# One-hot products of two tokens instead of four, in a gated Fourier and expert mixture

## The chip, the cores and the metric

The kernel runs on one core of a Trainium2 chip. A core has TensorE (matrix products into the PSUM banks), VectorE, ScalarE and GpSimd for work on elements, and queues that issue DMAs, most of them on SyncE (SP). Each engine works through its own list of instructions in order and waits on semaphores for the others. The metric is the device time of one execution in microseconds (us). Where a rate is compared, a product is one instruction of TensorE, with a weight load before it.

## The reference

The output mixes two branches with a gate for each token. Both work on the same x of 2048 tokens by 640.

```python
g = _sigmoid((x * gate_w).sum(-1, keepdims=True))
a = _A_ref(x, ...)      # Real(DFT over tokens of DFT over channels), as four products with matrices
b = _B_ref(x, ...)      # experts
return g * a + (1 - g) * b
...
# _B_ref, for each token and each of 32 heads
s1, s2 = q1 @ k1.T, q2 @ k2.T            # 16 scores each
# the two best of each, the two best of the four sums: 2 of 16*16 = 256 experts
g = _softmax(top_s, axis=-1)
act = _gelu(x @ u[top_e])
out = sum over h, k of g * act * v[top_e]
```

The kernel doesn't gather experts. It computes x times all 256 rows of u, and needs for each token and each expert the sum of the gates of those heads that chose it: a table G of 16 x 16 for each token. G is what the changed part makes.

## The kernel before

The kernel has one order of instructions, written out by its Python code. The main loop runs over 128 pieces of the product with the sequence matrices (2 matrices, 4 blocks of 512 tokens out, 16 blocks of 128 tokens in). A piece is 15 products of a 128x128 stationary block with 512 columns (five blocks of channels, and three products for each, since every operand is split into a high and a low half to keep precision; lines 143 to 145). After the pieces come 84 steps of the product with the hidden matrices, of much the same kind.

All else is background work. The class `Pump` holds generators; after every three products `run_bg(0.68)` adds 0.95 x 0.68 us of credit, and while the credit is positive the next step of a generator is issued. What a step yields is its planned cost on VectorE, and is taken off the credit. Other work on VectorE takes credit away too (`bg.credit -= ...`). So the order on VectorE and ScalarE, relative to TensorE's, comes from these costs. The code sets `early` (piece below 92), `ending` (the last seven pieces) and `closing` (the last piece of a block of 512 tokens) for the background to read.

In the first pieces the loop also makes weights (`w_part`, line 380: products with 32 columns of weights and 320 elements that write the four quarters of the partitions), then the scores and their best two. The choices end up in `ROWS[g]`, two tiles for the two halves of the tokens (g = 0 and 1): for each half three rows, namely the power of two that stands for the first index, the same for the second, and the gate weight, with 128 partitions for heads, choices and the two halves of a weight, and a column for a token. `put_rows` (line 721) copies the last rows there; up to then `last_rows` holds them in a tile with the tag `xl`, the place of x^T's low half.

`experts` (line 802) makes G from them. A set is 64 tokens; a half of the tokens has 16 sets. For a set, `build` (line 836) writes two tiles of 1024 columns in float16: pt, the one-hot vectors of the first index times the weight, and qt, those of the second index. That is two comparisons of the rows with a table of powers of two (`wtab4`, 16 powers each repeated for four tokens) and a product with the weight (line 845, 128 x 1024 elements each). Columns are ordered as block m, power e, token t: a block is four tokens, 64 columns.

`use` (line 848) then issues a burst: for each set and each block of four tokens one product pt^T qt of 64 x 64 (line 857). Blocks go to partitions 0 to 63 and 64 to 127 in turn, and a set fills one PSUM bank of eight times 64 columns. Of a product only the entries where both tokens are the same are wanted. `mask` (line 815) multiplies every fourth column by a mask that is zero on the partitions of other tokens, in four instructions of ScalarE for a set; `add_up` (line 821) adds four columns on VectorE into `cd[g]`. `settle` does both for one set at each step of the background. When a half is summed, `store_gates` (line 793) stores it with two DMAs, from which the last part loads G.

The tiles for four sets (`HOT`, two tiles of two sets) are allotted once the scores' tiles are given back. A group is three sets, or two under `ending`. The loop at line 864 builds sets while one is free, and issues the burst of the group before when none is. So the first set of the next group is built ahead of each burst. The second tile of `HOT` has the tag `WP` and is given up at piece 124. The tag `xl` is used again from piece 95 on, by `load_parts`.

Of the kernel before, what the change touches and what calls it, by code (L numbers as in the profile page):

```python
# [17 lines left out]
P = 128  # L18
# [3 lines left out]
E = 16  # L22
# [17 lines left out]
NSTEP = 7 * KZ  # L40
AHEAD = 5
AWAY = 11
BYPASS = 4
ACCUM_END = NT * (NC + 2) - 4

# [61 lines left out]
def gated_mix_kernel(ctx: ExitStack, tc: tile.TileContext, xT, xn, dreT, dimT, wsre, wsim, wq, kT, uT, vv, gw, out):  # L107
# [94 lines left out]


    banks = []
    p3, last_part, ending, closing, early, share = None, False, False, False, True, 0.95
    grow, staged, P22 = {}, {}, {}

    def load_row(q):
# [130 lines left out]
    wtab4 = const.tile([P, E, 4], F16)  # L339
    powers = const.tile([P, E], F16)  # L340
    top_bits = const.tile([P, 1], F32)
    mask4 = const.tile([P, 4], F32)

    def put_keys():
        for r in range(2):
# [6 lines left out]
    def make_tables():  # L352
        for e in range(E):
            nc.gpsimd.memset(powers[:, e:e + 1], 2.0 ** (E - 1 - e))
        nc.gpsimd.memset(top_bits, INF)
        nc.gpsimd.tensor_copy(wtab4, powers[:, :, None].to_broadcast([P, E, 4]))
        nc.vector.tensor_reduce(mask4, identf.rearrange("p (a b) -> p b a", b=4), op=OP.add, axis=AX.X)
        nc.vector.tensor_scalar(mask4, mask4, 1.0 / GSCALE, None, op0=OP.mult)

    for n, f in ((2, put_keys), (4, make_ident), (9, make_tables)):  # L360
        at(n, f)
# [430 lines left out]

    def store_gates(g):
        if g in summed and g not in stored:
            for s in range(2):
                nc.sync.dma_start(gd[g][s].rearrange("t e f m -> e t f m"), summed[g][64 * s:64 * s + 64])
            stored.add(g)

    free_sets = deque(range(4))
# [2 lines left out]
    def experts():  # L802


        shp = [P, 16, E, 4]
        wt = wtab4[:, None].to_broadcast(shp)
        todo = deque((g, c) for g in range(2) for c in range(16))
        cd = {}

        masked, unmasked = deque(), deque()  # L810

        def mask(t):
            f = t.rearrange("p m (e t) -> p (m e) t", t=4)
            for n in range(4):
                nc.scalar.activation(f[:, :, n], f[:, :, n], AF.Copy, scale=mask4[:, n:n + 1])  # L815

        def add_up(g, c, t):
            if c == 0:
                store_gates(g - 1)
                cd[g] = p3.tile([P, E, P], F32, name="cd", tag="cd")  # L820
            nc.vector.tensor_reduce(cd[g][:, :, 8 * c:8 * c + 8].rearrange("p e m -> p m e"),
                                    t.rearrange("p m (e t) -> p m e t", e=E), op=OP.add, axis=AX.X)
# [12 lines left out]

        def build(g, c, s):
            pt, qt = (HOT[s // 2][:, s % 2, n].rearrange("p (m e t) -> p m e t", e=E, t=4) for n in range(2))

            def row(n):
                r = ROWS[g][:, n, 8 * c:8 * c + 8, :].rearrange("p b (s t) -> p (b s) t", t=4)  # L840
                return r[:, :, None, :].to_broadcast(shp)

            assert rowed >= set(range(8 * g, 8 * g + 8))
            for o, a, b, op in ((pt, row(0), wt, OP.is_equal), (qt, row(1), wt, OP.is_equal), (pt, pt, row(2), OP.mult)):
                nc.vector.tensor_tensor(o, a, b, op=op)  # L845
                yield (0.8 if early else 1.05) + settle()

        def use(group):
            assert not last_part
            while masked or unmasked:  # L850
                yield settle(True)
            for i, (g, c, s) in enumerate(group):
                t = bank((6, 7, 5)[i], (P, 8, E * 4))
                pt, qt = (HOT[s // 2][:, s % 2, n].rearrange("p (m c) -> p m c", m=16) for n in range(2))
                for m in range(16):
                    r = slice(64 * (m % 2), 64 * (m % 2) + 64)
                    nc.tensor.matmul(t[r, m // 2, :], pt[:, m], qt[:, m], start=True, stop=True)  # L857
# [372 lines left out]
    prep_split = {NPC - 4: (0,), NPC - 3: (1,), NPC - 2: (2,), NPC - 1: (3, 4)}  # L1230
    WP = None
    for n in range(N0, NPC):
        ending, closing, early = n >= NPC - 7, n % NT == NT - 1, n < ACCUM_END
        seq_piece(n)
        follow(n)
        if n >= N1 and p3 is None and NT // NB - 1 in gated:
            p2_stack.close()
            p3 = ctx.enter_context(tc.tile_pool(name="p3", bufs=1, reuse_waits="tile"))
            pools.append(p3)
            HOT.append(p3.tile([P, 2, 2, 16 * E * 4], F16, name="hot0"))  # L1240
            HOT.append(p3.tile([P, 2, 2, 16 * E * 4], F16, name="hot1", tag="WP"))
            bg.add(experts(), late=True)
            bg.credit -= 3.0
        if n == NPC - 4:
            bg.drain(lambda: {2, 3} <= set(free_sets))
            HOT.pop()
# [57 lines left out]
```

## Time and profile before

| | us |
|---|---|
| median of 3 runs | 750.32 (749.74 to 750.33) |
| profiled execution | 750.43 |
| its span, first to last instruction | 748.7 |
| TensorE busy | 743.8 |
| VectorE busy | 585.7 |
| ScalarE busy | 365.9 |
| GpSimd busy | 342.4 |

The profile is of one execution. A group of instructions is given by its line, engine, operation, the tile written and those read, and their shape; then its count, its busy time, the mean time of one in ns, and the idle time of the engine before it with what ended it. A product's duration is the time from its start to its modelled end; products overlap, so their starts tell the pace. The granted clock of TensorE has a mean of 0.999 over the span.

### The profile page before, as it was taken

Reading aid. Unit: us, or ns where it says so; the run is one execution under the profiler, and the core shown is the slowest. Engines: PE = TensorE matmul, PEld = TensorE weight load, DVE = VectorE, ACT = ScalarE, POOL = GpSimd, SP = SyncE. Lnnn points to the kernel's source line nnn. Section 1 sums busy time; section 2 is a strip of 40 time slices with the busy share of each in tenths; the row PEclk is TensorE's granted clock in tenths of the full one; section 3 lists DMA queues with packets and bytes.
Section 4 is the critical chain, followed back from the end, with each engine's and each line's share of the span. In section 5 each row is a group of like instructions: output and inputs, shape, how many; then the busy total and the mean of one; then the engine's idle time right before and its main releaser. Section 6 shows DMA issues by size and latency. Waiting matters only on the chain.

```text
span 748.7 us, 11141 instructions
## 1 busy us (share of the span) xinstructions
PE 743.8 (99%) x3925; PEld 603.8 (81%) x3925; DVE 585.7 (78%) x741; ACT 365.9 (49%) x664; POOL 342.4 (46%) x286
## 2 busy tenths in 40 slices
PE   9999999999999999999999999999999999999998
PEld 7777767888888888888888888888888888888887
DVE  6964098495999899999999888979899974357651
ACT  4325234543544745555463686633545653443451
POOL 5533325440532424145235456643455793487253
PEclk9999999999999999999999999999999999999999
DMA  9999999777556786972398766488876689775301
GB/s 333 392 380 364 344 374 354 231 222 250 129 176 141 190 242 157 237 200 79 114 395 285 162 168 188 133 255 280 266 234 197 222 262 343 219 239 172 113 29 71
DMA packets 84488, 171.11 MB, mean 229 GB/s; under 512 B 16080, under 2 KB 21328, under 8 KB 84176
## 3 DMA queue, kind: packets, MB, share of 16 engines
q1 hardware_dynamic: 70960, 146.13, 57.9%
q0 software_dynamic: 5472, 9.96, 8.5%
q10 hardware_dynamic: 8000, 14.31, 5.2%
q8 instruction: 31, 0.51, 0.3%
q14 instruction: 25, 0.20, 0.1%
HBM read 136.40 MB, written 32.39 MB: 225 GB/s over the span
## 4 chain that ended last, share of the span: by engine, by line
PE 94%; DMA 5%; SPq 0%; DVE 0%; ACT 0%; issue 0%; ACTq 0%
PE b L143 30%; PE b L145 30%; PE b L144 30%; PE b L239 2%; DMA wf<-in_wsre 2%; PE b L380 2%; DMA wq<-in_wq 1%; PE b L857 1%; DMA xd<-X 1%; DMA gdr<-gc 1%; DVE wp L386 0%; SPq L177 0%; ACT WS L295 0%; ACTq L514 0%; DVE ST L1191 0%
## 5 line engine op out<-in xcount | busy, mean ns | idle before, releaser
L143 PE MATMUL b<-WS,X 128*128 128x512 f32 x620 | 243.3, 392 | 0.0
L144 PE MATMUL b<-WS,X 128*128 128x512 f32 x620 | 241.4, 389 | 0.0
L145 PE MATMUL b<-WS,X 128*128 128x512 f32 x620 | 241.3, 389 | 0.0
L139 POOL TENSOR_TENSOR WS<-wf,WS 128x512 fp32r<-128x512 f32 x89 | 131.9, 1486 | 168.3 <-ACT WS L138 151.8
L143 PEld LDWEIGHTS b<-WS,X 128*128 128x128 f32 x620 | 116.3, 188 | 28.2 <-issue 4.1
L145 PEld LDWEIGHTS b<-WS,X 128*128 128x128 f32 x620 | 116.4, 188 | 24.4
L144 PEld LDWEIGHTS b<-WS,X 128*128 128x128 f32 x620 | 116.4, 188 | 23.6
L138 ACT ACTIVATE WS<-wf 128x512 fp32r<-128x512 f32 x89 | 55.5, 626 | 69.0 <-PE b L145 40.9
L845 DVE TENSOR_TENSOR hot<-rows,wtab 128x1024 f16<-128x1024 f16 x64 | 57.8, 930 | 4.3 <-PE b L857 4.3
L139 POOL TENSOR_TENSOR xl<-xf,xh 128x640 fp32r<-128x640 f32 x16 | 27.2, 1702 | 72.0 <-ACT xh L138 72.0
L567 ACT ACTIVATE sc<-b 128x512 f32<-128x512 f32 x32 | 19.9, 621 | 80.8 <-PE b L145 77.0
L191 POOL DMA_DIRECT2D WS<-in_wsre x30 | 26.4, 881 | 61.8 <-ACT WS L189 60.5
L139 POOL TENSOR_TENSOR WS<-ra,WS 128x512 fp32r<-128x512 f32 x33 | 47.1, 1439 | 14.3 <-ACT WS L138 14.1
L815 ACT ACTIVATE b<-b,mask 128x128 f32<-128x128 f32 x128 | 43.1, 342 | 14.9 <-PE b L857 11.8
L138 ACT ACTIVATE WS<-ra 128x512 fp32r<-128x512 f32 x47 | 29.4, 631 | 42.4 <-PE b L145 29.6
L622 DVE TENSOR_TENSOR eq<-sc,mm 128x1024 f16<-128x1024 f32 x32 | 44.4, 1387 | 0.9
L629 DVE TENSOR_REDUCE tied<-eq 128x64 f32<-128x1024 f16 x32 | 39.0, 1219 | 0.9
L620 DVE TENSOR_REDUCE mm<-sc 128x64 f32<-128x1024 f32 x32 | 38.7, 1211 | 0.2
L139 POOL TENSOR_TENSOR WP<-ra,WP 128x512 fp32r<-128x512 f32 x13 | 19.2, 1490 | 31.0 <-ACT WP L138 30.9
L217 DVE SCALAR_TENSOR_TENSOR ST<-ST,grow 128x512 f32<-128x512 f32 x40 | 31.7, 855 | 1.7 <-ACT tw L138 1.7
L845 DVE TENSOR_TENSOR hot<-hot,rows 128x1024 f16<-128x1024 f16 x32 | 31.6, 986 | 0.0
L143 PE MATMUL b<-WU,xh 128*128 128x512 f32 x80 | 31.1, 389 | 0.0
(209 smaller groups left out, 1449.1 us busy)
## 6 DMA issues: line engine op xcount, KB each, us to landing
X<-xd SPq DMA_DIRECT2D x36, 640.0 KB, 6.5
wq<-in_wq SPq DMA_DIRECT2D x32, 640.0 KB, 7.1
wf<-in_wsim SPq DMA_DIRECT2D x64, 256.0 KB, 4.8
wf<-in_wsre SPq DMA_DIRECT2D x63, 256.0 KB, 6.4
ra<-pd SPq DMA_DIRECT2D x40, 256.0 KB, 3.3
pd<-ST ACTq DMA_DIRECT2D x35, 256.0 KB, 5.6
WS<-in_wsre POOLq DMA_DIRECT2D x30, 256.0 KB, 6.0
xd<-X SPq DMA_DIRECT2D x11, 640.0 KB, 9.1
```

Source lines behind the costliest of these rows:

```text
L138: nc.scalar.activation(h, f, AF.Copy)
L139: eng.tensor_sub(l, f, h.bitcast(F32))
L143: nc.tensor.matmul(o, wh, ah, start=first, stop=False, skip_group_check=more)
L144: nc.tensor.matmul(o, wh, al, start=False, stop=False, skip_group_check=more)
L145: nc.tensor.matmul(o, wl, ah, start=False, stop=last, skip_group_check=more)
L191: nc.gpsimd.dma_start(l, (wsre, wsim)[w][c, s], accum_op=OP.add)
L217: nc.vector.scalar_tensor_tensor(f, f, -1.0 if w else 1.0, g, op0=OP.mult, op1=OP.mult)
L620: nc.vector.tensor_reduce(m, sc, op=OP.max, axis=AX.X)
L622: nc.vector.tensor_tensor(eq, sc, m[:, :, None].to_broadcast([P, HH, E]), op=OP.is_equal)
L629: nc.vector.tensor_reduce(tied[:, s, ib, :], eq, op=OP.add, axis=AX.X)
L815: nc.scalar.activation(f[:, :, n], f[:, :, n], AF.Copy, scale=mask4[:, n:n + 1])
L845: nc.vector.tensor_tensor(o, a, b, op=op)
```

## The change

A block is now two tokens (`TB = 2`). Products are 32 x 32, go to the four quarters of the partitions in turn (`CG = 4`), and there are 32 of them for a set (`MS`). Two sets fill a bank; the banks 5, 6 and 7 are taken in rotation. A mask has two instructions for a bank, each over 256 elements, and one sum covers a bank. A group is four sets, and always an even number. The half's result lies in four strips of 32 partitions, which four DMAs store. The builds' planned cost is 0.85 for 0.8 in the early part.

`HOT` becomes a list of sets, and a fifth may be added by `free_now`. For the first half of the tokens it is a tile with the tag `xl`, if all 16 rows have been put in place and `late` is not set (`late`: from piece 86 on). For the second half it lies in the first half's rows, `ROWS[0]`, which are no longer read then.

```diff
+TB = 2
+MS = 64 // TB
+CG = P // (TB * E)
...
-        nc.gpsimd.tensor_copy(wtab4, powers[:, :, None].to_broadcast([P, E, 4]))
-        nc.vector.tensor_reduce(mask4, identf.rearrange("p (a b) -> p b a", b=4), op=OP.add, axis=AX.X)
+        nc.gpsimd.tensor_copy(wtab, powers[:, :, None].to_broadcast([P, E, TB]))
+        nc.vector.tensor_reduce(mask_t, identf.rearrange("p (a b) -> p b a", b=TB), op=OP.add, axis=AX.X)
...
-            for s in range(2):
-                nc.sync.dma_start(gd[g][s].rearrange("t e f m -> e t f m"), summed[g][64 * s:64 * s + 64])
+            for s in range(CG):
+                n, t = divmod(TB * s, 4)
+                nc.sync.dma_start(gd[g][n, t:t + TB].rearrange("t e f m -> e t f m"),
+                                  summed[g][TB * E * s:TB * E * (s + 1)])
...
-        shp = [P, 16, E, 4]
-        wt = wtab4[:, None].to_broadcast(shp)
+        shp = [P, MS, E, TB]
+        wt = wtab[:, None].to_broadcast(shp)
...
         def mask(t):
-            f = t.rearrange("p m (e t) -> p (m e) t", t=4)
-            for n in range(4):
-                nc.scalar.activation(f[:, :, n], f[:, :, n], AF.Copy, scale=mask4[:, n:n + 1])
+            f = t.rearrange("p m (e t) -> p (m e) t", t=TB)
+            for n in range(TB):
+                nc.scalar.activation(f[:, :, n], f[:, :, n], AF.Copy, scale=mask_t[:, n:n + 1])
...
-            nc.vector.tensor_reduce(cd[g][:, :, 8 * c:8 * c + 8].rearrange("p e m -> p m e"),
+            nc.vector.tensor_reduce(cd[g][:, :, 8 * c:8 * c + 16].rearrange("p e m -> p m e"),
                                     t.rearrange("p m (e t) -> p m e t", e=E), op=OP.add, axis=AX.X)
-            if c == 15:
+            if c == 14:
                 summed[g] = cd[g]
...
+        def free_now():
+
+            if todo[0][0] == 1:
+                if not HOT[4:] or HOT[4][0] == 0:
+                    if HOT[4:] and 4 not in free_sets:
+                        return [s for s in free_sets if s < 2 or not ending]
+                    if not HOT[4:]:
+                        HOT.append(None)
+                        free_sets.append(4)
+                    HOT[4] = 1, ROWS[0].rearrange("p a b c -> p (a b c)")[:, :16 * P].rearrange("p (n c) -> p n c", n=2)
+            elif not HOT[4:] and not late and len(rowed) == NT:
+                HOT.append((0, big.tile([P, 2, 16 * P // 2], F16, name="hot4", tag="xl")))
+                free_sets.append(4)
+            return [s for s in free_sets if s not in ((2, 3) if ending else (4,) if late and todo[0][0] == 0 else ())]
+
+        def pair(s):
+            f = HOT[s][1] if s == 4 else HOT[s]
+            return f[:, 0], f[:, 1]
...
-                yield (0.8 if early else 1.05) + settle()
+                yield (0.85 if early else 1.05) + settle()
...
             for i, (g, c, s) in enumerate(group):
-                t = bank((6, 7, 5)[i], (P, 8, E * 4))
-                pt, qt = (HOT[s // 2][:, s % 2, n].rearrange("p (m c) -> p m c", m=16) for n in range(2))
-                for m in range(16):
-                    r = slice(64 * (m % 2), 64 * (m % 2) + 64)
-                    nc.tensor.matmul(t[r, m // 2, :], pt[:, m], qt[:, m], start=True, stop=True)
-                unmasked.append((g, c, t))
+                if i % 2 == 0:
+                    t = bank(5 + rotate("hot", 3), (P, 16, E * TB))
+                    unmasked.append((g, c, t))
+                pt, qt = (f.rearrange("p (m c) -> p m c", m=MS) for f in pair(s))
+                for m in range(MS):
+                    r = slice(TB * E * (m % CG), TB * E * (m % CG + 1))
+                    nc.tensor.matmul(t[r, 8 * (i % 2) + m // CG, :], pt[:, m], qt[:, m], start=True, stop=True)
...
-            while todo and len(group) < (2 if ending else 3):
-                free = [s for s in free_sets if s < 2 or not ending]
-                if prev and (not free or ending and any(s > 1 for g, c, s in prev)):
+            while todo and (len(group) < (2 if ending else 4) or len(group) % 2):
+                free = free_now()
+                if prev and (not free or ending and any(s in (2, 3) for g, c, s in prev)):
                     yield from use(prev)
...
-        ending, closing, early = n >= NPC - 7, n % NT == NT - 1, n < ACCUM_END
+        ending, closing, early, late = n >= NPC - 7, n % NT == NT - 1, n < ACCUM_END, n >= NT * (NC + 2) - 10
```

`HOT` is filled with four sets of the same two tiles as before, and at piece 124 sets 2 and 3 are taken out of it.

More of the change, by code (lines that the diff above doesn't have):

```diff
@@ L204, in gated_mix_kernel @@
     banks = []
-    p3, last_part, ending, closing, early, share = None, False, False, False, True, 0.95
+    p3, last_part, ending, closing, early, late, share = None, False, False, False, True, False, 0.95
     grow, staged, P22 = {}, {}, {}
@@ L338, in gated_mix_kernel @@
     identf = p1.tile([P, P], F32, name="identf", tag="uf", bufs=2)
-    wtab4 = const.tile([P, E, 4], F16)
+    wtab = const.tile([P, E, TB], F16)
     powers = const.tile([P, E], F16)
     top_bits = const.tile([P, 1], F32)
-    mask4 = const.tile([P, 4], F32)
+    mask_t = const.tile([P, TB], F32)
     def put_keys():
@@ L834, in settle @@
             return us
+        def free_now():
[14 more added lines that the diff above has]
+            return f[:, 0], f[:, 1]
         def build(g, c, s):
-            pt, qt = (HOT[s // 2][:, s % 2, n].rearrange("p (m e t) -> p m e t", e=E, t=4) for n in range(2))
+            pt, qt = (f.rearrange("p (m e t) -> p m e t", e=E, t=TB) for f in pair(s))
             def row(n):
-                r = ROWS[g][:, n, 8 * c:8 * c + 8, :].rearrange("p b (s t) -> p (b s) t", t=4)
+                r = ROWS[g][:, n, 8 * c:8 * c + 8, :].rearrange("p b (s t) -> p (b s) t", t=TB)
                 return r[:, :, None, :].to_broadcast(shp)
@@ L1232, in gated_mix_kernel @@
     for n in range(N0, NPC):
-        ending, closing, early = n >= NPC - 7, n % NT == NT - 1, n < ACCUM_END
+        ending, closing, early, late = n >= NPC - 7, n % NT == NT - 1, n < ACCUM_END, n >= NT * (NC + 2) - 10
+        assert n < NT * (NC + 2) - 1 or not HOT[4:] or HOT[4][0] or 4 in free_sets
         seq_piece(n)
@@ L1239, in gated_mix_kernel @@
             pools.append(p3)
-            HOT.append(p3.tile([P, 2, 2, 16 * E * 4], F16, name="hot0"))
-            HOT.append(p3.tile([P, 2, 2, 16 * E * 4], F16, name="hot1", tag="WP"))
+            for t in ("hot0", "WP"):
+                f = p3.tile([P, 2, 2, 16 * E * 4], F16, name="hot", tag=t)
+                HOT.extend(f[:, a] for a in range(2))
             bg.add(experts(), late=True)
```

4 lines of the change are left out of this document (2 added, 2 removed).

## The prediction

> **What bounds the kernel now.** I read the page first, then the list of TensorE's waits, then the timeline around the one-hot products of line 857.
>
> ```profile
> span 748.7 us, 11141 instructions
> PE 743.8 (99%) x3925; PEld 603.8 (81%) x3925; DVE 585.7 (78%) x741; ACT 365.9 (49%) x664; POOL 342.4 (46%) x286
> PEclk9999999999999999999999999999999999999999
> PE 94%; DMA 5%; SPq 0%; DVE 0%; ACT 0%; issue 0%; ACTq 0%
> L845 DVE TENSOR_TENSOR hot<-rows,wtab 128x1024 f16<-128x1024 f16 x64 | 57.8, 930 | 4.3 <-PE b L857 4.3
> L815 ACT ACTIVATE b<-b,mask 128x128 f32<-128x128 f32 x128 | 43.1, 342 | 14.9 <-PE b L857 11.8
> ...
> PE b L326 <- PEq L1296: 0.8, 1, 0.8
> PE b L380 <- DMA wq<-in_wq: 0.7, 1, 0.7
> ```
>
> TensorE is busy for 99% of the span at the full granted clock, and the chain that ended last is 94% TensorE. A busy TensorE need not run at its peak, so the list of its waits matters more: 0.8 us at the start, 0.7 us in the weight products, and nothing after that. In the stretch that the change touches (410 to 600 us) TensorE waits for no one. What VectorE and ScalarE save there is off the path; only two things can move the end: the time that the one-hot products hold TensorE, and a new wait of TensorE.
>
> **What a burst costs.** The next rows are the timeline of TensorE around the first burst of three sets, then around the last of two; columns are start, duration, line, form and count. The two rows under them are all products of line 857.
>
> ```profile
> 419.09 0.39 PE L144 MATMUL b<-WS,X 128*128 128x512 f32 x1
> 419.32 0.39 PE L145 MATMUL b<-WS,X 128*128 128x512 f32 x1
> 419.64 0.95 PE L857 MATMUL b<-hot 128*64 128x64 f16 x48
> 420.52 0.50 PE L143 MATMUL b<-WS,X 128*128 128x512 f32 x1
> 420.85 0.39 PE L144 MATMUL b<-WS,X 128*128 128x512 f32 x1
> ...
> 586.79 0.39 PE L145 MATMUL b<-WS,X 128*128 128x512 f32 x1
> 587.10 0.69 PE L857 MATMUL b<-hot 128*64 128x64 f16 x32
> 587.73 0.50 PE L143 MATMUL b<-WS,X 128*128 128x512 f32 x1
> 588.07 0.39 PE L144 MATMUL b<-WS,X 128*128 128x512 f32 x1
> ...
> L857 PEld LDWEIGHTS <-hot x512: 106/113/113, 419.6 to 587.6; 128*64 128x64 f16 x171
> L857 PE MATMUL b<-hot x512: 196/196/217, 419.6 to 587.6; 128*64 128x64 f16 x171
> ```
>
> Large products start 0.23 us apart. From the L145 before the first burst to the L144 after it are 1.53 us; without the burst these two starts would be 2 x 0.227 = 0.45 us apart, so a burst of 48 costs 1.08 us. The last, of 32, costs 1.28 - 0.45 = 0.83 us. The difference, 0.25 us, is 16 products: 15.7 ns a product, 31.4 ns for the two that lie side by side in the halves of the partitions. What is left, 1.08 - 48 x 0.0157 = 0.33 us, is paid once a burst, at the switch to small products and back. The 512 products are ten bursts of 48 and one of 32: 10 x 1.08 + 0.83 = **11.63 us**. This is all that the change can work on.
>
> **The new bursts.** 32 sets in fours make eight bursts. A set is now 32 products of 32 x 32 columns in place of 16 of 64 x 64, four side by side in the quarters of the partitions. No row shows such a product, so I bound four of them. If all the time is in columns, four take half of 31.4 ns: 15.7 ns. If what sets 31.4 ns is a fixed time for each strip, they take 31.4 ns. If the supply of instructions sets it, the only rate that the rows prove is 15.7 ns for a weight load and a product, so four take 62.8 ns. That four strips do overlap shows at line 380:
>
> ```profile
> 40.98 0.39 PE L145 MATMUL b<-WS,X 128*128 128x512 f32 x1
> 41.30 2.36 PE L380 MATMUL b<-wq,kp 128*32 128x320 f32 x32
> 43.59 0.50 PE L143 MATMUL b<-WS,X 128*128 128x512 f32 x1
> 43.93 0.40 PE L144 MATMUL b<-WS,X 128*128 128x512 f32 x1
> ```
>
> Here 2.95 - 0.45 - 0.33 = 2.17 us for 32 products 32 columns wide, 68 ns each for 320 elements; one large product spends 0.227 x 320 / 512 = 142 ns on as many. So strips of 32 run at least two at a time, and the switch in and out looks the same as for strips of 64 (43.59 to 43.93 as 420.52 to 420.85). I take the middle of the first two cases, 23.6 ns, as an estimate. A burst of four sets is 32 fours: 0.33 + 32 x 0.0236 = 1.09 us, eight are 8.7 us: **-2.9 us**. The ends are 8 x (0.33 + 0.50) = 6.7 us (-4.9), 8 x (0.33 + 1.00) = 10.7 us (-1.0) and 8 x (0.33 + 2.01) = 18.7 us (+7.1). The change breaks even at 11.63 / 8 - 0.33 = 1.12 us for 32 fours, 35 ns a four. A ninth burst, should the last sets come after the switch to groups of two, is +0.33.
>
> [...]
>
> **Masks, sums, tables.** The masks go from 128 instructions over 128 elements to 32 over 256; the sums from 32 to 16, each still over 512 elements.
>
> ```profile
> L567 ACT ACTIVATE sc<-b 128x512 f32<-128x512 f32 x32 | 19.9, 621 | 80.8 <-PE b L145 77.0
> L821 DVE TENSOR_REDUCE cd<-b x32: 678/681/696, 422.3 to 592.5; 128x128 f32<-128x512 f32 x32
> core 0: us, PE busy (x) PEld busy (x) DVE busy (x) ACT busy (x) POOL busy (x), PEclk, DMA share, GB/s
> 410.00:600.00 190.00, 190.00 (x1299) 155.56 (x1298) 172.13 (x217) 110.38 (x248) 101.56 (x73) 1.00 0.69 210
> L622 DVE TENSOR_TENSOR eq<-sc,mm 128x1024 f16<-128x1024 f32 x32 | 44.4, 1387 | 0.9
> ```
>
> A mask of 256 lies between 342 ns (128) and 621 ns (512): 0.43 us, 14 us in all for 43. VectorE loses 16 x 0.68 = 11 us. Both are worth nothing at the end, since TensorE doesn't wait there; they move the last sets earlier. The three comparisons and products of a set (line 845) keep their 1024 elements, in runs of two instead of four. I count no change; the other bound is the one-by-one 1.39 us of L622 against the free-running 0.68, +0.7 us x 96 = 68 us on an engine with 190 - 172 = 18 us free. The smaller tables are made in piece 9, beside the large products, as before. `store_gates` issues four DMAs for two.
>
> ```profile
> L796 SPq DMA_DIRECT2D gd<-cd x4: 527/547/637, 487.4 to 616.8; - x4
> L177 SPq DMA_DIRECT2D wf<-in_wsim x64: 327/382/1322, 316.0 to 572.8; - x64
> ```
>
> That is 2 x 0.55 us more on SP, once with the loads of `wf` queued behind it; these are issued five pieces (5 x 15 x 0.227 = 17 us) ahead. Cost nothing; uncovered, 1.1 us.
>
> **The fifth set, and the wait it should prevent.** With four sets and bursts of three, the set after the burst was built before the burst was issued, so VectorE had one set's lead. With four sets and bursts of four there is none: the burst stands right behind the last build. `free_now` gives a fifth set in the first half only when all 16 rows are in place and `late` is still off, that is before piece 86.
>
> ```profile
> 422.71 2.53 ACT L246 ACTIVATE ST<-b 128x512 f32<-128x512 f32 x5
> ...
> 452.60 0.63 ACT L189 ACTIVATE WS<-WS 128x512 fp32r<-128x512 f32 x1
> 453.14 1.93 ACT L721 ACTIVATE rows<-lb 128x384 f16<-128x384 f16 x1
> ...
> 420.52 0.68 DVE L845 TENSOR_TENSOR hot<-hot,rows 128x1024 f16<-128x1024 f16 x1
> ...
> 467.58 0.95 PE L857 MATMUL b<-hot 128*64 128x64 f16 x48
> ...
> 468.95 0.68 DVE L845 TENSOR_TENSOR hot<-hot,rows 128x1024 f16<-128x1024 f16 x1
> ```
>
> The copies at 422.71 empty the banks after piece 79, so piece 80 starts near 424.1 us, and piece 86 six pieces and two bursts later, near 424.1 + 6 x 3.4 + 2.2 = 446.7. The last row is copied at 453.14, behind a split (452.60) that piece 87 issues at about 450. So I expect that **the place in x^T's low half is never used**, and that the first half, four bursts, runs without a spare set. In the second half the first rows are the spare, and the lead is as before.
>
> What a missing lead costs is VectorE's lag. The first four sets were ready at 420.52 + 0.68 = 421.20; their burst would be issued about 0.6 us later than the first one now (12 builds cost 0.05 more in the pump's credit, over a share of 0.95), reaching its fourth set near 419.64 + 0.6 + 0.7 = 420.9: 0.3 us of waiting. The first 16 sets were ready at 469.63, 2.05 us after the burst at 467.58; less the same 0.7 and what the missing sums give back, about 0.5. Between them VectorE was less far behind. I take **+0.8 us** for the four; bounds 0 and 4 x 2.05 = 8.2. Behind a waiting product stands all of TensorE's queue, so such a wait is paid in full.
>
> **Sum.** Profiled execution: span 748.7 of 750.43 us, with 1.7 us around it. 748.7 - 2.9 + 0.8 = 746.6, and 748.3 us with what lies around; the median of the runs, 750.32, is 0.1 below the profiled one, so **748.2 us**.
>
> **Rivals.**
> Strips don't shrink: four still take 31.4 ns, since product and load have a fixed time. Gain 1.0 - 0.8 = 0.2: 750.1 us. For it: nothing in the trace is faster than 31.4 ns in one strip. Against: 15.7 ns is short enough that a part must be columns.
> VectorE's lag takes the gain: the bursts at 420 and 468 wait the whole 1.56 and 2.05 us by which the sets were late in the old schedule, and the others little: 3.6 - 2.9 = +0.7, 751.0 us. It decides once the waits pass 2.9 us. For it: no lead in the first half. Against: 11 us less work on VectorE.
> Slower, by the supply of instructions: a burst is now 256 instructions (128 loads and products) instead of 96, and if the sequencer's pace is what the 15.7 ns show, a burst takes 2.34 us: +7.1, 757.4 us. It decides from 35 ns a four, 4.4 ns an instruction. For it: nothing in the rows proves a faster pace. Against: 48 products run at the pace of 32, so the pace isn't running dry within 96 instructions.
> [...]
> Runs of two halve VectorE's pace: 68 - 18 - 11 = 39 us of waiting, near 787 us.
>
> **How the numbers follow.** Forecast (fours between 15.7 and 28 ns, waits under 1.5 us): 0.50, its own range 745.4 to 748.8. Strips that don't shrink: 0.18. VectorE's lag: 0.13. Supply of instructions: 0.13. A floor for every product: 0.03. Halved pace: 0.03. A measurement of this kernel tells about 0.2% (1.5 us) from no change. Faster by more than that is the forecast, 0.50; within it the second case and a third of the lag's, 0.22; slower the rest, 0.28. The range goes from the forecast's low end, 745.4, up over the lag to 753.5; above it lie most of the supply's case and the last two, 0.17.
>
> **What would show it.** Right: eight rows of 128 products of 128x32 at line 857's successor, each about 0.95 us long with 0.33 around it; no TensorE wait over 1 us on `hot`; masks of 256 elements, 32, and 16 sums; no build in the low half's place. Wrong: bursts over 1.5 us, a list of waits in which TensorE waits for VectorE's `hot` by more than 3 us, or builds near 1.3 us where GpSimd is idle.

## The result, and the profile after

| | before | after |
|---|---|---|
| median of nine runs, us | 750.33 (749.74 to 751.02) | 753.14 (750.83 to 756.03) |
| profiled execution, us | 750.43 | 753.41 |
| its span, us | 748.7 | 751.6 |
| cost of all bursts (line 857, after it 883), waits in them included, us | 11.64 | 13.08 |

The ratio is 1.0039, with a 95% interval of 1.0021 to 1.0057: the change makes the kernel 2.9 us slower (1.6 to 4.3). The forecast was 748.2, faster; the time lies inside the range of 745.4 to 753.5, on the wrong side of the start.

First rows of the page of after, then its busy times from 410 to 600 us (PE, PEld, DVE, ACT, POOL, each with its count, then the granted clock), then the groups of masks and sums:

```profile
PE 743.5 (99%) x4437; PEld 604.1 (80%) x4437; DVE 580.2 (77%) x725; ACT 337.8 (45%) x568; POOL 343.3 (46%) x286
PE 91%; DVE 4%; DMA 3%; ACT 1%; SPq 1%; issue 0%; DVEq 0%; ACTq 0%
```

```profile
410.00:600.00 190.00, 188.30 (x1805) 154.93 (x1804) 164.52 (x201) 80.22 (x147) 102.50 (x73) 1.00 0.70 210
```

```profile
L826 DVE TENSOR_REDUCE cd<-b 128x256 f32<-128x512 f32 x16 | 11.0, 687 | 12.2 <-ACT b L820 10.2 <-DMA gd<-cd 2.0
...
L820 ACT ACTIVATE b<-b,mask_t 128x256 f32<-128x256 f32 x32 | 14.5, 466 | 13.4 <-PE b L883 12.8
```

VectorE has lost 7.6 us of work in this stretch (172.13 before) and ScalarE 30 us (110.38 before), and yet VectorE now stands on the chain that ended last, with 4% where it had 0%; TensorE's part has gone from 94% to 91%. TensorE, which was busy for all 190 us, now stands still for 1.7 of them. Its list of waits says for whom:

```profile
PE b L883 <- DVE hot L869: 1.7, 2, 1.4
PE b L383 <- DMA wq<-in_wq: 1.6, 2, 1.0
PE b L329 <- PEq L1323: 0.8, 1, 0.8
PE b L242 <- ACT WS L298: 0.4, 1, 0.4
```

The first line is new. Next, TensorE's timeline around the third burst, which waits for nothing, and the fourth, the last of the first half. Under it are all products of line 883 that read `HOT`: least, median and longest duration in ns.

```profile
452.91 0.39 PE L148 MATMUL b<-WS,X 128*128 128x512 f32 x1
453.23 1.25 PE L883 MATMUL b<-hot 128*32 128x32 f16 x128
454.40 0.50 PE L146 MATMUL b<-WS,X 128*128 128x512 f32 x1
454.74 0.39 PE L147 MATMUL b<-WS,X 128*128 128x512 f32 x1
...
469.27 0.39 PE L148 MATMUL b<-WS,X 128*128 128x512 f32 x1
469.59 0.68 PE L883 MATMUL b<-hot 128*32 128x32 f16 x64
470.54 0.38 PE L883 MATMUL b<-hot 128*32 128x32 f16 x32 [0.27 <-DVE hot L869]
472.34 0.37 PE L883 MATMUL b<-hot 128*32 128x32 f16 x32 [1.43 <-DVE hot L869]
472.65 0.50 PE L146 MATMUL b<-WS,X 128*128 128x512 f32 x1
472.98 0.39 PE L147 MATMUL b<-WS,X 128*128 128x512 f32 x1
```

```profile
L883 PE MATMUL b<-hot x896: 176/184/190, 421.7 to 568.3; 128*32 128x32 f16 x180
```

Counted as the prediction counted a burst, the third costs 454.74 - 452.91 - 0.45 = **1.38 us**. So do five others, to 0.03. The fourth costs 472.98 - 469.27 - 0.45 = 3.26, of which 1.88 us are waits for VectorE's builds; the first costs 1.57, with a wait of 0.19. Eight bursts without a wait would be 11.05 us, 0.6 less than before; with the waits they are 13.08.

The pace inside a burst can be read from the same rows. A group lasts from its first start to its last end, and a product lasts 0.18 us. After the long wait, 31 steps take 0.37 - 0.18 = 0.19 us: 6.3 ns a step, 25 ns for four products. In the third burst 127 steps take 1.25 - 0.18 = 1.07 us: 8.4 ns, 33.7 ns for four. So fours run at 25 ns at first and then more slowly. The single starts of the third burst show it too: from the first product of a strip to the next 39 ns, then six steps of 25, which makes 28 products in the four strips (all 32 after the long wait), then one step of 29 to 44, and from there on 33 to 38, but for one step of about 57 ns where the third set begins and one where the fourth does. Between these steps a product with its load takes about 8.3 ns, 4.15 ns an instruction.

The span has grown by 2.9 us: -0.6 from bursts without waits, +2.1 from the two waits; the rest, some 1.4, is waits in the first 120 us (the lines of L383 and L242: 2.0 us in place of 0.7), where nothing was changed but the size of two tables; the experiments tell whether they belong to the change.

**Why the fourth burst waits.** The next rows are the timeline of ScalarE, VectorE and GpSimd ahead of it; times in brackets are idle times and what ended them.

```profile
454.15 0.63 ACT L191 ACTIVATE WS<-wf 128x512 fp32r<-128x512 f32 x1 [3.63 <-DMA wf<-in_wsim]
...
455.35 1.91 ACT L724 ACTIVATE rows<-lb 128x384 f16<-128x384 f16 x1
456.76 2.10 ACT L820 ACTIVATE b<-b,mask_t 128x256 f32<-128x256 f32 x4
...
458.05 0.69 DVE L826 TENSOR_REDUCE cd<-b 128x256 f32<-128x512 f32 x1 [3.05 <-ACT b L820]
...
459.86 3.56 DVE L869 TENSOR_TENSOR hot<-rows,wtab 128x1024 f16<-128x1024 f16 x2
463.35 1.77 DVE L869 TENSOR_TENSOR hot<-hot,rows 128x1024 f16<-128x1024 f16 x1
465.04 3.75 DVE L869 TENSOR_TENSOR hot<-rows,wtab 128x1024 f16<-128x1024 f16 x2
468.71 1.77 DVE L869 TENSOR_TENSOR hot<-hot,rows 128x1024 f16<-128x1024 f16 x1
470.41 1.28 DVE L869 TENSOR_TENSOR hot<-rows,wtab 128x1024 f16<-128x1024 f16 x2
471.61 0.68 DVE L869 TENSOR_TENSOR hot<-hot,rows 128x1024 f16<-128x1024 f16 x1
472.21 2.36 DVE L869 TENSOR_TENSOR rows<-rows,wtab 128x1024 f16<-128x1024 f16 x2
...
459.61 1.57 POOL L142 TENSOR_TENSOR DD<-draw,DD 128x640 fp32r<-128x640 f32 x1 [2.85 <-ACT DD L141]
461.14 3.43 POOL L142 TENSOR_TENSOR WS<-wf,WS 128x512 fp32r<-128x512 f32 x2
464.53 2.02 POOL L142 TENSOR_TENSOR DD<-draw,DD 128x640 fp32r<-128x640 f32 x1
466.50 3.43 POOL L142 TENSOR_TENSOR WS<-wf,WS 128x512 fp32r<-128x512 f32 x2
```

Two things come together. ScalarE waits 3.63 us for a load of `wf`; the copy of the last rows and the masks are behind that wait, and VectorE stands idle for 3.05 us at the sum. Then the builds of the burst's last three sets, nine in number, take from 459.86 to 472.29, 12.4 us: the first six last about 1.8 us each while GpSimd's splits (L142) run from 459.61 to 469.93, and at 470.41, when GpSimd has stopped, they are back at 0.68. The last build ends at 472.29, and the last 32 products of the burst start at 472.34.

The burst doesn't lack a spare set. The build at 472.21 writes into the first rows: it is the next set's, and in the code it stands ahead of the burst. But it is a lead on paper, since VectorE is behind its plan: without a wait TensorE would be at the fourth set 96 products after 469.59, by estimate (96 x 8.4 ns) at about 470.4, and that set is ready at 472.29.

### The profile page after: what moved, and what is told of

Its sections match the earlier page's. It is cut to its first block, busy times and chain, and to the rows that moved or that the text cites. A ratio compares the mean times of both kernels' runs of the same rounds, so it can differ in the third digit from the quotient of the medians.

```text
span 751.6 us, 12054 instructions
## 1 busy us (share of the span) xinstructions
PE 743.5 (99%) x4437; PEld 604.1 (80%) x4437; DVE 580.2 (77%) x725; ACT 337.8 (45%) x568; POOL 343.3 (46%) x286
## 4 chain that ended last, share of the span: by engine, by line
PE 91%; DVE 4%; DMA 3%; ACT 1%; SPq 1%; issue 0%; DVEq 0%; ACTq 0%
PE b L146 29%; PE b L147 29%; PE b L148 29%; DVE hot L869 2%; PE b L242 2%; DMA wq<-in_wq 2%; PE b L383 2%; PE b L883 1%; SPq L719 1%; DMA wf<-in_wsim 1%; ACT rows L724 1%; DVE ST L220 1%; DMA wf<-in_wsre 0%; DVE WU L142 0%; DVE tw L142 0%
## 5 line engine op out<-in xcount | busy, mean ns | idle before, releaser
L142 POOL TENSOR_TENSOR WS<-wf,WS 128x512 fp32r<-128x512 f32 x89 | 131.6, 1483 | 172.4 <-ACT WS L141 169.4
L869 DVE TENSOR_TENSOR hot<-rows,wtab 128x1024 f16<-128x1024 f16 x56 | 60.7, 1117 | 2.5 <-PE b L883 2.5
L142 POOL TENSOR_TENSOR xl<-xf,xh 128x640 fp32r<-128x640 f32 x16 | 27.2, 1706 | 73.1 <-ACT xh L141 66.6
L142 POOL TENSOR_TENSOR WS<-ra,WS 128x512 fp32r<-128x512 f32 x33 | 46.6, 1422 | 15.3 <-ACT WS L141 10.4
L142 POOL TENSOR_TENSOR WP<-ra,WP 128x512 fp32r<-128x512 f32 x13 | 19.2, 1491 | 31.0 <-ACT WP L141 30.9
L146 PE MATMUL b<-WU,xh 128*128 128x512 f32 x80 | 31.1, 389 | 0.0
L147 PE MATMUL b<-WU,xh 128*128 128x512 f32 x80 | 31.1, 389 | 0.0
L148 PE MATMUL b<-WU,xl 128*128 128x512 f32 x80 | 31.1, 389 | 0.0
L220 DVE SCALAR_TENSOR_TENSOR ST<-ST,grow 128x512 f32<-128x512 f32 x40 | 29.7, 797 | 1.4 <-DMA grow<-gdr 0.8
```

What stands on the lines that cost most here:

```text
L142: eng.tensor_sub(l, f, h.bitcast(F32))
L146: nc.tensor.matmul(o, wh, ah, start=first, stop=False, skip_group_check=more)
L147: nc.tensor.matmul(o, wh, al, start=False, stop=False, skip_group_check=more)
L148: nc.tensor.matmul(o, wl, ah, start=False, stop=last, skip_group_check=more)
L220: nc.vector.scalar_tensor_tensor(f, f, -1.0 if w else 1.0, g, op0=OP.mult, op1=OP.mult)
```

## The experiments

The kernel of after, and of before, run once more, frame the rest: `again` and `again_b` are the changed kernel unaltered, `old_again` the one before.

> The changed kernel once more, unaltered, for a second profile. If the waits for VectorE's builds are a property of the schedule, the fourth burst again waits 1.5 to 2.5 us and the span is again near 751.6 us. If they come from how long a few transposes and loads happen to take, the wait moves by more than 1 us, to another burst or to none, and the span moves with it; the eight bursts without waits still cost 1.38 us each (11.05 us in all). If the waits for the weight loads before 125 us (1.4 us more than in the profile of before) belong to the change, they are here again; if they are chance, they are not.

> The changed kernel unaltered, a second time, on the chip of the held one. Theory: 751.5 to 753.5; wait at the fourth burst of 0.9 to 1.9 us, bursts 12.2 to 13.1 us in all. If the early waits at the weight products are part of the change they are again 1.3 us or more in excess; if they are chance they may be anything from 0.5 to 2.5. A run near 755 to 756 would be one with a granted clock of 0.998.

> The kernel before once more, unaltered, for a second profile of it. If the short waits in the first 125 us (start, and the weight loads) are chance, they differ from those of the first profile by some tenths of a us up to 1 us here too, while the eleven bursts cost the same 11.64 us and TensorE waits for no build.

`again`: 752.32 us in one run (before, beside it, 750.41). The fourth burst waits again, 0.98 us, the first 0.33; all others cost 1.38. `again_b`: 752.43 us (750.80 to 756.79, 12 runs; before 750.45; ratio 1.0039, 1.0022 to 1.0055); the fourth burst costs 3.37, the first 1.56. `old_again`: 750.41, the same eleven bursts of 11.64 us in all, and no wait for a build. So the wait at the fourth burst belongs to the change, and its size differs between 1.0 and 2.0 us from run to run. The early waits for `wq` come and go: 1.6 us in the first profile of the changed kernel, 1.0 in `again`, none in `again_b`, and 0.7 and 0.5 in the two of the kernel before. TensorE's waits in `again_b`:

```profile
PE b L883 <- DVE hot L869: 1.8, 2, 1.4
PE b L329 <- PEq L1323: 0.8, 1, 0.8
```

**`twos`, half the burst.** Groups of two in the first half of the tokens, four after it.

```diff
-            while todo and (len(group) < (2 if ending else 4) or len(group) % 2):
+            while todo and (len(group) < (2 if ending or todo[0][0] == 0 else 4) or len(group) % 2):
```

> Groups of two sets in the first half, of four in the second; two sets are then built ahead of each burst of the first half. Eight bursts of 64 products and four of 128. Theory 'VectorE is late, and a burst's first 28 or so products take 25 ns a four, the others 33': 0.85 us for a burst of 64, 8 x 0.85 + 4 x 1.38 = 12.3 us, no waits in the first half, 751.0 us. Rival 'every four takes 33 ns': 0.33 + 0.53 = 0.86 us, no difference here. Rival 'the waits come from elsewhere than the lack of lead': waits of 1 to 2 us remain, 752 to 753 us.

Measured: 751.22 us against 750.41 (ratio 1.0010, 1.0001 to 1.0020). No wait for a build. Bursts of 64 products cost 0.81 us, those of 128 1.38; twelve bursts are 11.95 us. Shorter bursts give VectorE its lead back, at the price of 2 x 0.81 - 1.38 = 0.24 us for every burst that is cut in two.

**`ones`, a quarter.** One set at a time with 1.5 of credit in between, so that large products stand ahead of each.

```diff
                     nc.tensor.matmul(t[r, 8 * (i % 2) + m // CG, :], pt[:, m], qt[:, m], start=True, stop=True)
+                if i % 2:
+                    unmasked.append((g, c0, t))
+                if i < len(group) - 1:
+                    yield 1.5
```

> Each burst is cut into bursts of one set, with at least three large products between them, so that TensorE's queue can fill again. Theory 'after some 30 products the supply of instructions sets the pace': all eight fours of a set run at 25 ns, a burst of 32 costs 0.33 + 0.20 = 0.53 us, 32 of them 17.0 us, +5.4 on before: 755.7 us. Rival 'the second pace belongs to the products (their bank, their strips)': fours at 33 ns from the start or from the second set of a bank, 0.60 us a burst, 19 us in all, 757.7 us.

The timeline of TensorE in `ones`, around one burst of 32:

```profile
443.46 0.39 PE L148 MATMUL b<-WS,X 128*128 128x512 f32 x1
443.78 0.38 PE L882 MATMUL b<-hot 128*32 128x32 f16 x32
...
444.42 0.39 PE L147 MATMUL b<-WS,X 128*128 128x512 f32 x1
```

It costs 0.96 - 0.45 = 0.51 us: every step is 25 ns, (0.38 - 0.18) / 31 x 4. The same products that run at 33 ns in the middle of a burst of 128 run at 25 in a burst of 32 behind large products. So does the second set of a bank (0.52 us). This speaks against a property of the products or of their place in a bank. That the supply of instructions sets the second pace, and that a queue fills again in between, is the author's reading: no run changed the supply, and no row shows the queue. The time of 772.8 says nothing of that: the delays pushed six sets to the end, where a burst of 192 waits for its builds and costs 16.4 us.

**`later`, all bursts of the first half held back.**

```diff
+            if group[0][0] == 0:
+                yield 5.0
             for i, (g, c, s) in enumerate(group):
```

> In the first half of the tokens every burst is issued 5 us of planned time after the last build of its group; nothing else changes. Theory 'VectorE is late': no wait of TensorE for the builds in the first half, all bursts at 1.38 us, so 11.05 against 11.63 us of before: 749.7 us, and the spread between runs as narrow as that of before (under 1.5 us). Rival 'the small products cost more than the clean bursts show' or 'the loss lies outside the bursts': stays at 752 to 753 us.

Measured: 764.95 us (ratio 1.0193, 1.0170 to 1.0215). The first seven bursts cost 1.38 and wait for nothing, as the theory has it. But the delays add up: the last burst starts at 596.5 in place of 567.5, waits for its builds and costs 13.8 us, and 3.8 us more pass behind it in a wait for a sum. For the total neither side of the expectation held: both the 749.7 us of the theory and the 752 to 753 us of its rivals are far too low.

**`sums_later`, the sums out of the way.** A masked bank is left for two more steps before VectorE sums it.

```diff
-            if masked:
-                add_up(*masked.popleft())
+            if masked and masked[0][3] > 0 and not force:
+                masked[0] = masked[0][:3] + (masked[0][3] - 1,)
+            elif masked:
+                add_up(*masked.popleft()[:3])
...
-                masked.append(unmasked.popleft())
+                masked.append(unmasked.popleft() + (2,))
```

> The changed kernel, but a sum is listed on VectorE at least three builds after its masks were listed on ScalarE, in place of one; the planned costs and the places of the bursts stay. Theory 'VectorE stands still behind a sum whose masks are late, and so falls 6 us behind before the fourth burst': its idle time before the sums falls from 10 us to under 5, the builds of the fourth burst end 2 to 3 us earlier, its wait is gone or under 0.5 us, bursts 11.1 to 11.5 us in all, 749.8 us and a spread under 2 us. Rival 'the lag comes from the slow builds beside GpSimd alone': the builds that take 1.77 us stay as many, the wait stays at 1 to 2 us, 751.5 to 753 us.

Measured: 751.21 us against 750.21 (ratio 1.0007, 0.9997 to 1.0017). This interval and those of the unaltered kernel don't meet, by a narrow margin, so the late sum is a part of the loss. Theory and rival each have half of it: the wait gets smaller but doesn't go, and the median lies between their two times. In its profile VectorE's idle time before sums falls from 10.2 to 4.7 us and the fourth burst waits 0.85 us (0.98, 1.88 and 1.99 in the three profiles of the unaltered kernel); the slow builds are there as before.

That profile is of the slowest of its eleven runs, 754.05 us at a granted clock of 0.997, and what made it slow is not at the fourth burst. TensorE's timeline:

```profile
108.75 0.75 PE L383 MATMUL b<-wq,kp 128*32 128x320 f32 x8 [2.09 <-DMA wq<-in_wq]
...
109.92 0.63 PE L147 MATMUL b<-WS,X 128*128 128x512 f32 x1
110.34 0.63 PE L148 MATMUL b<-WS,X 128*128 128x512 f32 x1
```

Behind an early wait of 2.09 us for `wq`, large products start 0.43 us apart instead of 0.23 up to 112.9 us, and the granted clock from 109 to 114 us is 0.66. Behind the fourth burst of this run, which waited 0.85 us, they start 0.23 us apart.

**`hurry`, VectorE later in the first half**: the early builds' planned cost is 0.65 for 0.85, so that bursts are issued earlier while builds take as long as ever.

> The changed kernel with 0.65 in place of 0.85 as the planned cost of a build in the early part, so that VectorE is given its work faster and the bursts follow their builds sooner: the suspected lag is made larger. Theory 'waits of TensorE for VectorE at the bursts': waits of 2 to 4 us each at the first, third and fourth burst, bursts 16 to 20 us in all, 756 to 760 us, and a granted clock under 1 where a wait is longest. Rival 'the loss isn't in these waits': 752 to 753 us as the changed kernel.

Measured: 757.70 us (ratio 1.0098, 1.0084 to 1.0112), with waits at the first burst, which costs 4.14 us, and at the third, which costs 3.25. The fourth, expected to wait too, costs 1.38. What comes behind the first is more than the wait. TensorE's timeline of `hurry`, and its busy times from 421 to 426 us:

```profile
419.54 0.38 PE L883 MATMUL b<-hot 128*32 128x32 f16 x32 [1.15 <-DVE hot L869]
421.34 0.38 PE L883 MATMUL b<-hot 128*32 128x32 f16 x32 [1.43 <-DVE hot L869]
...
422.46 0.63 PE L146 MATMUL b<-WS,X 128*128 128x512 f32 x1
422.89 0.63 PE L147 MATMUL b<-WS,X 128*128 128x512 f32 x1
```

```profile
421.00:426.00 5.00, 4.66 (x44) 3.75 (x45) 5.00 (x9) 1.60 (x4) 0.00 (x0) 0.66 0.20 56
```

Eight large products start 0.43 us apart instead of 0.23, at a granted clock of 0.66 over these 5 us: another 8 x 0.2 = 1.6 us.

**`old_three`, the kernel before without its lead**: three sets for groups of three (`free_sets = deque(range(3))`, and the drain at piece 124 asks for set 2 alone).

> The kernel before, with three places for sets in place of four, so that no set is built ahead of a burst; products of four tokens and groups of three as they were. Theory 'the lead of one set hides VectorE's lag': the bursts near 420 and 468 wait 1 to 2 us each and those near 505 as well, 12.5 to 15 us for the bursts, 752 to 754 us. Rival 'the waits belong to bursts of 128 products': no waits, 750.4 us.

Measured: 760.09 us (ratio 1.0136, 1.0118 to 1.0154). Three bursts of the first half wait, and cost 3.29, 4.84 and 2.95 us; six to nine large products some 0.43 us apart follow each wait. The lead is worth far more in the old kernel than expected, and the new one gives up less of it than this does.

**`spare`, the low-half place opened to the end of the pieces that may use it**: `late` from piece 92 in place of 86.

> The changed kernel with the limit for the place in x^T's low half moved from piece 86 to piece 92, so that the fifth set of the first half is used once, for the first set of the fourth burst. Theory 'the unused place was not what was missing': its builds wait on VectorE for ScalarE's copy of the last row out of that place, near 457 us, so VectorE is as late as before at the fourth burst: waits of 1 to 2 us, 752 to 753.5 us. Rival 'a set built ahead of the third burst mends it': no wait at the fourth burst, 750.2 us.

Measured: 752.21 us (ratio 1.0023, 1.0009 to 1.0037). The fourth burst costs 2.84. A further spare set doesn't help by more than can be told: the theory held, it isn't the number of sets that is short there.

**`both`, sums later and two bursts held**: the edit of `sums_later`, and 2.0 of credit ahead of the first and the fourth burst.

> sums_later, and 2 us of planned time ahead of the first and the fourth burst alone (the two that waited). Theory 'all that is lost is lost in waits for VectorE at these two bursts': no wait of TensorE for the builds, bursts 11.1 us in all against 11.64, so 749.7 to 750.1 us and a spread as that of before: no slower than before, and by too little faster to be told. Rival 'something else of the change costs time': 751 us or more with bursts at 11.1.

Measured: 754.77 us (ratio 1.0053, 1.0040 to 1.0066). The bursts are as expected, free of waits and 11.10 us in all; the time is not, 4.7 us above the upper end of what was expected. TensorE's timeline:

```profile
454.35 0.39 PE L146 MATMUL b<-WS,X 128*128 128x512 f32 x1
457.34 0.50 PE L147 MATMUL b<-WS,X 128*128 128x512 f32 x1 [2.60 <-DMA WS<-in_wsim]
...
458.00 1.26 PE L887 MATMUL b<-hot 128*32 128x32 f16 x128
```

The delay at the first burst moved the third from 453.23 to 458.00, behind the start of the next piece, whose low half of a stationary block wasn't there yet. In after no product waits there. Two things differ. The third burst, 1.38 us of small products, no longer covers the transfer; and GpSimd issued that transfer at 451.82 in place of 448.50, behind a split that had waited 6.26 us for ScalarE (2.65 in after) and took 3.81 us (2.13). By estimate the burst in its old place would have covered its 1.38 of the 2.60 us, about half; why GpSimd was later wasn't traced further.

**`hold`, only the fourth burst held.**

```diff
+            if group[0][:2] == (0, 12):
+                yield 3.0
             for i, (g, c, s) in enumerate(group):
```

> After with the fourth burst alone held back by 3.0 in the pump's credit (some 3.2 us); sums, tables and the first three bursts stay where they are. Theory (the burst is 1.38 us where TensorE's instructions keep up at 4.15 ns each, and what the change lost on top of that is VectorE being late at two places): no wait on `hot` at the fourth burst, eight bursts between 11.1 and 11.4 us, the third still ahead of piece 88 so that no product waits for WS; median 750.4 to 751.2, 1 to 2 us below the run of the changed kernel beside it. Rival (a delay only moves the wait on, as it did where all first-half bursts were held): a wait of 1 us or more at a later burst or at WS, median at or above that of the changed kernel. Rival (the early waits at the weight products are part of the change, 0.6 us or more): waits there of 1.2 us or more again, median above 751.2 although the bursts sum to 11.2.

Measured: **750.31 us** (749.43 to 751.27, 11 runs), a tenth below the expected stretch, with before at 750.45 (ratio 0.9998, 0.9989 to 1.0007) and the changed kernel at 752.43 on the same chip. TensorE's whole list of waits, and its timeline around the fourth burst:

```profile
PE b L329 <- PEq L1325: 0.8, 1, 0.8
```

```profile
470.57 0.39 PE L148 MATMUL b<-WS,X 128*128 128x512 f32 x1
470.89 1.25 PE L885 MATMUL b<-hot 128*32 128x32 f16 x128
...
472.41 0.39 PE L147 MATMUL b<-WS,X 128*128 128x512 f32 x1
```

The fourth burst costs 1.38, all eight 11.14. Moving one burst by some 3 us takes back the whole loss, and only the place was changed: in `hold` the nine builds ahead of the burst take 12.4 us as in after (456.40 to 468.82) and are ready 2 us before it. `hold` also keeps the new tables, masks, sums and stores, so none of these costs anything that can be told; its profile has no early wait for `wq` at all. No version is faster than the kernel before by more than can be told: what is left of the change is 11.14 - 11.64 = -0.5 us of products, and the interval of `hold` reaches from -0.8 to +0.5 us.

The wait may cost more than its 1.0 to 2.0 us. Of the 21 runs of the changed kernel (nine, and twelve of `again_b`) eight took 753.8 to 756.8 us at a granted clock of 0.995 to 0.998; the other 13 had 0.999 or 1.0. This fits the spell of half pace that follows a wait in `hurry` and `old_three` (large products 0.43 us apart, for 0.23). None of those eight runs was profiled, so where their spell stands was not seen. For the fourth burst speak the kernels without a wait there: all eleven runs of `hold`, all ten of `twos` and all 66 of the kernel before beside the experiments had 0.999 or 1.0. Against it speaks `sums_later`, the one profiled run of this kind, whose spell follows the early wait for `wq`. How many of the eight belong to which stays open.

## Why the prediction was wrong

**What bounds the kernel: right.** TensorE's products and its waits decide. The 30 us that ScalarE lost and the 7.6 us of VectorE bought nothing; even `hold`, without any wait for them, is no faster than before.

**The cost of the new bursts: the mechanism half right, the size wrong.** This is the first step that failed: "I take the middle of the first two cases, 23.6 ns, as an estimate", a burst of 1.09 us, -2.9 in all. Measured: 1.38 us, -0.6, close to the far end that the text gave (-1.0). The switch was right: 0.51 - 8 x 0.025 = 0.31 us a burst, for 0.33. A four takes 25.0 ns in the first 28 to 32 products of a burst, near the estimate. After that it takes 33 ns, 4.15 ns an instruction, and columns and a fixed time don't account for it, since the same products run at 25 ns in `ones`. The estimate weighed columns against a fixed time for a strip, and left the supply of instructions to a rival. That rival names a cause that fits both paces, though no run shows it by itself, and its own break-even, 4.4 ns an instruction, was missed by 0.25; its price of 7.9 ns came from a row that doesn't show the fastest pace of instructions, since a load and a product now take 8.3 ns together where they took 15.7. The text's argument against it ("48 products run at the pace of 32") shows at most that the pace doesn't change within 96 instructions at 7.9 ns each, not that 256 instructions at 3 ns each could be had.

**Waits for VectorE: the places right, size and cause wrong.** The first and the fourth burst were named. The wait at the first costs 0.18 to 0.33 us, for 0.3. That at the fourth costs 1.0 to 2.0 for "about 0.5", and this is the second step that failed. It was derived from the missing spare set; but the fourth burst has one. What was not in the working is that VectorE is late on its own: a sum behind ScalarE's wait for `wf`, and nine builds of which six take 2.6 times their duration beside GpSimd (1.8 us for 0.68). Both could be seen before: the timeline of the old kernel has builds of 1.78 and 1.95 us at 463 to 466, and its sums wait 10.9 us for masks; of the builds the prediction read only the free-running 0.68. `sums_later` shows that the late sum is a part of it, `spare` that a further spare set is worth nothing that can be told (752.21, by the unaltered 752.43), and `hold` that the whole of the loss hangs on this one burst's place. In after, `again`, `again_b` and `hold` the builds ahead of the fourth burst take 1.8 us as long as GpSimd's splits run and 0.68 us once these pause; but no run took GpSimd's work away, so that it is the cause is a reading and not shown.

**Busy times counted at nothing, rightly:** masks (14.5 us for the 14 worked out), sums (11.0, half of before), the tables, two more stores, and builds in runs of two, which take 0.68 us where GpSimd is idle. The low half's place was never used, as expected: the last row is copied at 455.35, after piece 86.

**The sum.** Predicted -2.9 + 0.8 = -2.1; measured in the profiled run -0.6 + 2.1, and 1.4 of early waits, which are chance: they are absent in `again_b`, and in `hold`, which keeps all of the change but one burst's place. Over the runs the loss is 2.9 us, a ratio of 1.0039 in both sets: the waits, the half pace (0.43 us a large product for 0.23) that seems to follow some of them, and the small gain. One more sum of the prediction doesn't hold: the forecast's own range was to end at 748.8 us, but its conditions, fours of up to 28 ns (1.8 us gained) and waits of up to 1.5 us, reach to 750.0.

**The rivals.** "Strips don't shrink" has the bursts nearly right (10.7 us for 11.05), "VectorE's lag" has the waits nearly right in kind (up to 3.6 us). Each was priced with the other's term at the forecast's value. They hang on different things and could both be true, as they were; both together, -1.0 + 3.6, come to +2.6 us, 752.9. That this is near the measured 753.14 is in part luck, for the profiled run has -0.6 and 2.1, and the rest is the early waits. The chances treated them as alternatives. "A floor for every product", which the chances count with 0.03, is shown by no run: in a burst without waits, 1.38 us, 128 products start 8.4 ns apart on the mean. "Halved pace" didn't occur: builds in runs of two take 0.68 us where GpSimd is idle, not 1.39.

## What to carry to other kernels

Here the rate of small products, 25 ns for four, held only for the first 28 to 32 of a burst and was 33 ns after; before making a burst longer, ask whether its rate holds to its end. The fourth burst stood right behind the builds that feed it, and their slowest stretch (six builds of 1.8 us, for 0.68) set its wait of 1.0 to 2.0 us and not their mean, so read the feeder's timeline for that stretch and place the burst by it: here issuing one burst 3 us later took the changed kernel from 752.43 to 750.31 us, all that the change had lost. And a delay was not free either: `later` (764.95 us) and `both` (754.77 us) have all or nearly all of their bursts free of waits, and lose more than that at other places.

## What the runs showed of the hardware

A wait of TensorE cost more than its length in some runs: in `hurry` 2.58 us of waits at the first burst were followed by another 1.6 us at half pace. These rows of `old_three` are around the shortest single wait that was seen to be followed by half pace:

```profile
476.61 0.44 PE L857 MATMUL b<-hot 128*64 128x64 f16 x16 [1.67 <-DVE hot L845]
...
478.44 0.63 PE L145 MATMUL b<-WS,X 128*128 128x512 f32 x1
478.87 0.63 PE L143 MATMUL b<-WS,X 128*128 128x512 f32 x1
```

After 1.67 us of idleness large products start 0.43 us apart (478.44 to 478.87); after 0.27 and 1.43 us in after's fourth burst they start 0.23 us apart, at a granted clock of 1.00 from 473 to 478 us. Two waits of 1.15 and 1.43 us close together were followed by it (`hurry`), and single ones of 1.79 and 3.20 us (`old_three`) and 2.09 us (`sums_later`). But length alone doesn't decide: after the 2.60 us of the profiled run of `both` the granted clock stays at 1.00, and large products start 0.23 us apart. (Its other four runs had 0.998.) What decides it was not shown.

Also unexpected: the three DMA transposes of the last rows take SP 5.52 us to issue in after and 4.97 in `again_b`, against 3.65 before, and the loads of `wf` for which ScalarE waits stand behind them. `twos` has 3.69. `hold` has 5.23 and is as fast as before, so it costs nothing where the fourth burst is held; whether it makes the wait there longer wasn't tested, and its cause wasn't found.
